# Gated values summed in place, output weights summed at their conversion, and the second FFN's operands loaded ahead of its first products

## The chip, the cores and the metric

The kernel runs on one core of a Trainium2 chip. A core has TensorE (PE, the matmuls), VectorE (DVE), ScalarE (ACT), GpSimd (POOL) and SyncE (SP, which here only issues DMAs), a scratch memory of 128 partitions (SBUF) and eight accumulation banks (PSUM). The metric is the device time of one execution in microseconds, as the median of some runs.

## The reference

The kernel computes three layers in a row, in float32:

```python
x = attention(q, k, v)              # 4 x 8 heads x 576 rows, window of 128, ALiBi bias -> x [2304, 512]
gate = 1 / (1 + exp(-(x @ w_gate))) # w_gate, w_val: [512, 1536]
val = x @ w_val
y = (gate * val) @ w_out            # w_out: [1536, 512]
# then a mixture of 8 experts, each token goes to the best one
out[mask] = gate_w[mask, None] * (relu(y[mask] @ w1[e]) @ w2[e])
```

w_gate, w_val and w_out arrive as 64-bit floats and are turned into 32-bit ones on the chip. Each float32 matmul operand is split into a high part and a low part (a rounding copy on ACT, a subtraction on DVE), and each product is three matmuls: high by high, high by low, low by high.

## The kernel before

The work comes in stages: attention; the first FFN matrices (gate and val) for a first pair of token chunks, interleaved with attention; the same for a second pair of chunks, called stage B here; the product with w_out; routing; the experts.

Stage B runs from about 290 to 440 us. It loops over 12 slices f of the 1536 hidden columns. For each f the 2 x 2 block product over the pair of chunks is done with seven products instead of eight (a Strassen form, lines 496 and on: m1 to m7), each of them six matmuls of 128 x 128 by 128 x 512. The seven products need sums of the token blocks (made once, held in 14 buffers) and, for each f, the weights W and sums of the weights T. Both come back from DRAM (`load_wt`, line 391), and are split by `split_w` (line 404): a cast to `wh` on ACT, then the subtraction on DVE, which writes the low part into the loaded buffer `wt`. In iteration f the weights of f + 1 are split and those of f + 2 are loaded. In the same iteration w_out's block f - 1 is converted (`split_wo`, line 740, by `split64`, line 136): an ACT multiplication, three integer operations on DVE, a store of the 32-bit block to DRAM (`wo_d`) by POOL's queue, and a split that stays in SBUF for the products to come.

The results of an iteration are gated in `keep_g` (line 441): `(tanh + 1) * val` on DVE, for two halves (chunks). For each pair of slices (f even, f odd; index kk) there are four blocks of gated values, A11 and A21 from the even f, A12 and A22 from the odd one. The product with w_out is again a seven-product form for these chunks, so POOL forms S1 = A21 + A22, S2 = S1 - A11, S3 = A21 - A11, S4 = A12 - S2, and seven blocks are stored to DRAM (`g7_d`) by POOL's queue. Before, the blocks and sums take four buffers for each kk: `gq` of the even f, `gq` of the odd f, and two of `sq`.

Buffers: nearly all of these operands are taken from one pool of 33 slots of 128 x 1024 floats (`NSLOT`, line 41, `slot(...)`), each given back when its last reader is done; a DMA or an engine that needs a slot waits for one. Smaller temporaries (`row(...)`) come from a pool of 10 rows of 128 x 528 floats (`NMID`, line 48). In stage B an iteration takes rows for c11, r1, c22 and c21 (the results of the products on their way to the gate) and one for w_out's block in conversion.

The order of the work: the program is written as Python loops, and a planner puts each engine's instructions in an order by their place in the program, their operands and free buffers, as it computes them ahead; every engine and queue then works strictly in that order. Where the code says `tc.manual_schedule(engines={...})`, the named engines keep the order of the program. Before, PE does so in the whole loop of stage B (line 805).

After stage B follows the product with w_out. The tokens of rows 4 and 3 (`ROWS = [4, 3, 2, 1, 0]`, 256 tokens each) go first, as plain products `mm2` with operands `gl`, `gh` (loaded from `gT_d`, split by `split_g`). Then `strassen` (line 1245) does the seven-product form for the second pair of chunks, in the order A11, S1, S2, S3, A22, S4, A12, with operands `ol`, `oh` (`load_op`, `split_op`) and the sums T of w_out (`tl`, `th`). Before, `prepare` (line 1282) brings these in: behind the products of row 4 it loads three of the six pairs of w_out blocks back from `wo_d`, sums them on POOL (four subtractions of 128 x 256 for each pair, line 1174), splits the sums, and loads the first operand; behind row 3 it does the other three pairs, then splits the first operand, loads the second and splits it.

A block of zeros (`zrow`, line 831) is stored to five places of the token table `x2_d` by POOL's queue at f = 3.

Of the kernel before, what the change touches and what calls it, by code (L numbers as in the profile page):

```python
# [9 lines left out]
F32 = mybir.dt.float32  # L10
F32R = mybir.dt.float32r
# [4 lines left out]
ALU = mybir.AluOpType  # L16
# [6 lines left out]
NT = B * S  # L23
DM = 512
FF = 1536
# [35 lines left out]
def attn_ffn_moe(ctx: ExitStack, tc: tile.TileContext, qkd, vd, wgv, w_out, emb, tau, w1, w2, cst, ids, out):  # L61
# [6 lines left out]
    wo_d = dram.tile([FF, DM], F32, tag="wo_d", name="wo_d")  # L68
# [49 lines left out]
    def lo_sub(eng, o, i, h):  # L118
        e = nc.vector if eng == "v" else nc.gpsimd
        e.tensor_tensor(out=o, in0=i, in1=h.bitcast(F32), op=ALU.subtract)  # L120
# [12 lines left out]
        nc.vector.scalar_tensor_tensor(out=yi, in0=hi, scalar=-2 ** 31, in1=yi, op0=ALU.bitwise_and,  # L133
                                       op1=ALU.bitwise_or)

    def split64(raw, wh, wl, nm, e2, keep):
        y = row(f"cv{nm}")[:, 0:512]
        conv64_a(raw, y)
        conv64_b(raw, y)
        nc.gpsimd.dma_start(keep, y)  # L140
        hi_copy("a", wh, y)
        lo_sub(e2, wl, y, wh)


    edge_pad = ctx.enter_context(tc.tile_pool(name="pad", bufs=1, side="right"))
# [245 lines left out]
    def load_wt(f):  # L391
        if f < KF:
            for z, (d, src) in list(enumerate(((wf, wf_d), (tf, tf_d))))[:1 if f < NC else 2]:
                t = slot([P, 2 * KD, P], F32R, f"wt{z}_{f}")
                d[f] = t.bitcast(F32)
                w_lo[f, z] = t
                nc.sync.dma_start(flat(d[f]), src[f * P:(f + 1) * P, :])
# [37 lines left out]
    gq, sq = {}, {}  # L435

    def g7_rows(name, kk, n=1):
        r = (NAMES.index(name) * KF // 2 + kk) * P
        return g7_d[r:r + n * P, :]

    def keep_g(f, half, gate, val):
        kk, odd = divmod(f, 2)
        if f not in gq:
            gq[f] = slot([P, 2, 512], F32, f"gq{f}")
        o = gq[f][:, half, :]
        nc.vector.scalar_tensor_tensor(out=o, in0=gate, scalar=1.0, in1=val, op0=ALU.add, op1=ALU.mult)  # L446
        if odd or not half:
            nc.gpsimd.dma_start(g7_rows(f"A{half + 1}{odd + 1}", kk), o)  # L448

        def put(name, t, x, y, op):  # L450
            nc.gpsimd.tensor_tensor(out=t, in0=x, in1=y, op=op)
            nc.gpsimd.dma_start(g7_rows(name, kk), t)

        a = gq[f - odd]
        if not odd and not half:
            sq[kk] = [slot([P, 2, 512], F32, f"sq{z}_{kk}") for z in range(1)]
            put("S3", sq[kk][0][:, 0, :], a[:, 1, :], a[:, 0, :], ALU.subtract)
        elif odd and half:
            sq[kk].append(slot([P, 2, 512], F32, f"sq1_{kk}"))
            put("S1", sq[kk][0][:, 1, :], a[:, 1, :], o, ALU.add)  # L460
            put("S2", sq[kk][1][:, 0, :], sq[kk][0][:, 1, :], a[:, 0, :], ALU.subtract)
        elif odd:
            put("S4", sq[kk][1][:, 1, :], o, sq[kk][1][:, 0, :], ALU.subtract)

    def piece(mm, ev):
        def both():
# [261 lines left out]

    op_ = ctx.enter_context(tc.tile_pool(name="op", bufs=8, side="right", reuse_waits="tile"))
    wo = []  # L730
    wo_raw = {}

    def load_wo(j):
        if j >= KF:
            return
        t = slot([P, 1024], I32, f"wor{j}")
        nc.sync.dma_start(t, w_out[j].bitcast(I32))
        wo_raw[j] = t

    def split_wo(j):  # L740
        if j % 3 == 0:
            wo.append(tuple(op_.tile([P, 3, DM], F32R, tag="c", name=f"wo{z}_{j}") for z in range(2)))
        h_, l_ = wo[-1]
        split64(wo_raw.pop(j), h_[:, j % 3, :], l_[:, j % 3, :], f"wo{j}", "v", wo_d[j * P:(j + 1) * P, :])

    def rnorm(ss, n, nm, w=P):
        s0 = sm.tile([P, n], F32, tag=f"sa{n}", name=f"sa_{nm}")[0:w, :]
# [54 lines left out]
    sv[0]["m2"]()  # L802
    bB["S3+"]()
    bB["S3"]()
    with tc.manual_schedule(engines={ENG.PE}):
        for f in range(KF):
            s, t = sv[f], sv[f + 1] if f + 1 < KF else None
            s["m5"]()
            if f == 0:
                bB["A22"]()  # L810
                bB["S4+"]()
            if f + 1 < NC:
                sum_w(f + 1, store=False)
            split_w(1, f + 1, 0)
            s["m6"]()
            if f == 0:
                bB["S4"]()
            if t:
                t["m1"]()
            s["m7"]()  # L820
            split_w(1, f + 1, 1)
            if t:
                t["m2"]()
            load_wt(f + 2)
            s["m4"]()
            if f:
                split_wo(f - 1)
            load_wo(f + 1)
            s["m3"]()
            if f == 3:  # L830
                zrow = row("zrow")
                nc.gpsimd.memset(zrow, 0.0)
                nc.gpsimd.dma_start(x2_d[NT:NT + 1, :], zrow[0:1, :])
                for b in LATE:
                    for u in range(2):
                        nc.gpsimd.dma_start(x2_d[(2 * b + u) * P:(2 * b + u + 1) * P, :], zrow)
            elif f == 7:
                load_emb()
            elif f == 9:
                norm_emb()  # L840
            elif f == 10:
                turn_emb()
    split_wo(KF - 1)


# [42 lines left out]
    idt = cp.tile([P, E * TCOL], I32, tag="idt", name="idt")  # L888
    nc.gpsimd.memset(idt, NT)
    nc.sync.dma_start(tab_d.rearrange("(p c) o -> p (c o)", p=P), idt)  # L890
    split_g(ROWS[0])
    tri = cp.tile([P, P], BF16, tag="tri", name="tri")
    nc.vector.tensor_copy(tri, tri_f)
# [268 lines left out]
    wt2 = {}  # L1162

    def load_w2(kk):
        t = slot([P, 2, DM], F32, f"wo32_{kk}")
        nc.sync.dma_start(t, wo_d[2 * kk * P:2 * (kk + 1) * P, :].rearrange("(z p) d -> p z d", p=P))
        wt2[kk] = t

    def sum_w2(kk):
        w = wt2.pop(kk)  # L1170
        b11, b12, b21, b22 = w[:, 0, 0:256], w[:, 0, 256:512], w[:, 1, 0:256], w[:, 1, 256:512]
        t = slot([P, 4, 256], F32, f"tq_{kk}")
        for z, (x, y) in enumerate(((b12, b11), (b22, t[:, 0, :]), (b12, b22), (b21, t[:, 1, :]))):
            nc.gpsimd.tensor_tensor(out=t[:, z, :], in0=x, in1=y, op=ALU.subtract)
        h_, l_ = (slot([P, 4, 256], F32R, f"t{z}_{kk}") for z in "hl")
        hi_copy("a", h_, t)
        lo_sub("v", l_, t, h_)
        wt2[kk, "T"] = h_, l_

    def w2_of(name, kk, z):  # L1180
        i = int(name[1:])
# [366 lines left out]
```

## Time and profile before

| | us |
|---|---|
| median of 3 runs | 894.05 |
| lowest, highest | 891.28, 894.74 |
| the profiled execution | 892.74 |
| its span (first to last instruction) | 890.8 |
| mean granted TensorE clock, share of full speed | 0.952 |

| engine | busy us | share of the span |
|---|---|---|
| PE | 816.2 | 92% |
| DVE | 595.3 | 67% |
| ACT | 459.3 | 52% |
| POOL | 264.2 | 30% |

A busy share is a mean over stages with different limits. Matmuls overlap, so a busy PE isn't PE at its peak. The granted clock is what TensorE ran at, as a share of its full 2.4 GHz. A wait is put down to the event that came last before the waiting instruction. In a row of the timeline "SPq" and "POOL ... DMA" are issues of DMAs; a DMA lands later.

### The profile page before, as it was taken

What the parts mean: (1) busy time and instruction counts of PE and PEld (TensorE: products, weight loads), DVE (VectorE), ACT (ScalarE), POOL (GpSimd) and SP (SyncE); (2) the same over time, 40 slices, a digit from 0 to 9 for tenths busy, and PEclk for the clock granted to TensorE, in tenths of its full rate; (3) what the DMA queues carried; (4) which work ended last, traced back from release to release, by engine and by line L of the source; (5) the groups of instructions that cost most, each with busy time, mean ns of one, the idle gap of its engine ahead of it and who ended that gap; (6) DMA issues with size and microseconds to landing.
All of it is one profiled execution on the core that took longest, in us unless ns stands there. A gap on an engine that the chain in (4) does not pass through costs nothing. (4 is left out here: it accounts for less than half of the span.)

```text
span 890.8 us, 15647 instructions
## 1 busy us (share of the span) xinstructions
PE 816.2 (92%) x5563; PEld 670.0 (75%) x5563; DVE 595.3 (67%) x1392; ACT 459.3 (52%) x956; POOL 264.2 (30%) x378
## 2 busy tenths in 40 slices
PE   9989999999999778786769699999899999999997
PEld 6768878888887556565557478777788999898796
DVE  7998787777997756676683566574574744645721
ACT  6897666665565323334343556873543543444410
POOL 6775322320001442334392210233122301210300
PEclk9999999999999878797879799999899999999999
DMA  8685656454535664563844358424348744544300
GB/s 272 188 280 190 231 192 207 154 184 171 210 120 215 209 214 138 192 208 123 294 165 137 113 177 278 170 73 157 93 130 272 274 166 145 188 171 137 132 22 17
DMA packets 68191, 156.13 MB, mean 175 GB/s; under 512 B 9191, under 2 KB 23271, under 8 KB 68112
## 3 DMA queue, kind: packets, MB, share of 16 engines
q1 hardware_dynamic: 58256, 125.59, 42.1%
q0 software_dynamic: 9856, 29.53, 9.2%
q8 instruction: 44, 0.72, 0.3%
q14 instruction: 35, 0.29, 0.1%
HBM read 110.96 MB, written 44.79 MB: 175 GB/s over the span
## 5 line engine op out<-in xcount | busy, mean ns | idle before, releaser
L1106 PE MATMUL h<-xe,weh 128*128 128x256 f32 (+4 forms) x512 | 107.7, 304 | 0.0
L116 POOL TENSOR_SCALAR p<-p,rs 128x192 f32<-128x192 f32 x140 | 76.3, 562 | 101.2 <-DVE rs L267 51.9
L1124 PE MATMUL z<-weh,h 128*128 128x512 f32 (+3 forms) x320 | 101.7, 397 | 0.9 <-DVE h L1109 0.6
L904 PE MATMUL y<-wo,gh 128*128 128x512 f32 x240 | 80.5, 407 | 11.1 <-ACT gh L104 11.1
L120 DVE TENSOR_TENSOR wel<-wer,weh 128x1024 fp32r<-128x1024 f32 x64 | 77.1, 1220 | 14.6 <-ACT weh L104 7.0
L1106 PEld LDWEIGHTS h<-xe,weh 128*128 128x128 f32 x512 | 85.8, 194 | 1.3 <-DVE h L1109 0.2
L1106 PE MATMUL h<-xe,wel 128*128 128x256 f32 (+4 forms) x256 | 77.7, 304 | 0.0
L251 ACT ACTIVATE p<-p,mx 128x192 f32<-128x192 f32 x144 | 64.0, 446 | 24.2 <-DVE mx L248 23.9
L104 ACT CAST weh<-wer 128x1024 fp32r<-128x1024 f32 x64 | 66.4, 1049 | 12.2 <-PE z L1124 9.7
L1129 POOL DMA_INDIRECT out<-y,cols x19 | 22.3, 1172 | 169.7 <-DVE y L1128 159.0
L1108 ACT ACTIVATE h<-h 128x256 fp32r<-128x256 f32 (+4 forms) x64 | 26.7, 417 | 81.3 <-PE h L1106 79.5
L1124 PEld LDWEIGHTS z<-weh,h 128*128 128x128 f32 (+3 forms) x320 | 56.6, 181 | 15.6 <-DVE h L1109 1.0
L448 POOL DMA_DIRECT2D g_d<-gq x18 | 10.3, 572 | 177.8 <-DVE gq L446 177.8
L1124 PE MATMUL z<-wel,h 128*128 128x512 f32 (+3 forms) x160 | 62.7, 392 | 0.0
L904 PEld LDWEIGHTS y<-wo,gh 128*128 128x128 f32 x240 | 45.7, 193 | 22.3 <-ACT gh L104 11.5
L1109 DVE SCALAR_TENSOR_TENSOR h<-h,h 128x256 fp32r<-128x256 f32 (+4 forms) x64 | 29.5, 463 | 47.0 <-ACT h L1108 46.8
L1106 PEld LDWEIGHTS h<-xe,wel 128*128 128x128 f32 x256 | 49.7, 194 | 0.0
L904 PE MATMUL y<-wo,gl 128*128 128x512 f32 x120 | 47.8, 399 | 1.8 <-DVE gl L120 1.8
L1128 DVE TENSOR_SCALAR y<-z,xg 128x512 f32<-128x512 f32 (+3 forms) x22 | 16.4, 747 | 49.2 <-PE z L1124 49.2
L1020 POOL DMA_INDIRECT tab_d<-ids_sb,ai x18 | 22.5, 1249 | 62.3 <-DVE xr L978 23.3
L527 DVE TENSOR_TENSOR c<-c,c 128x512 f32<-128x512 f32 x22 | 15.1, 686 | 33.7 <-ACT c L526 33.7
L248 DVE CUSTOM_DVE_ANT_0 p<-s,bias 128x192 f32<-128x192 f32 x96 | 30.6, 350 | 8.4 <-PE s L237 8.4
(450 smaller groups left out, 2264.5 us busy)
## 6 DMA issues: line engine op xcount, KB each, us to landing
wer<-in_w SPq DMA_DIRECT2D x64, 512.0 KB, 5.4
wr<-in_wgv SPq DMA_DIRECT2D x24, 512.0 KB, 5.3
qk<-in_qkd SPq DMA_DIRECT2D x36, 320.0 KB, 3.6
ol<-g_d SPq DMA_DIRECT2D x21, 512.0 KB, 4.0
gl<-gT_d SPq DMA_DIRECT2D x15, 512.0 KB, 8.6
v<-in_vd SPq DMA_DIRECT2D x36, 192.0 KB, 3.5
wf_d<-wf SPq DMA_DIRECT2D x12, 512.0 KB, 2.6
wt<-wf_d SPq DMA_DIRECT2D x12, 512.0 KB, 3.6
```

Source lines behind the costliest of these rows:

```text
L104: nc.scalar.copy(o, i)
L116: nc.gpsimd.tensor_scalar(out=t, in0=t, scalar1=r, scalar2=0.0, op0=ALU.mult, op1=ALU.add)
L120: e.tensor_tensor(out=o, in0=i, in1=h.bitcast(F32), op=ALU.subtract)
L248: nc.vector.tensor_tensor_reduce(out=o, in0=ss[u][:, j * WK:(j + 1) * WK], in1=bias, scale=-0.125, scalar=3.0e38, op0=ALU.add, op1=ALU.min ...
L251: nc.scalar.activation(out=o, in_=o, func=AF.Exp, scale=-1.0, bias=mx[:, z:z + 1], accum_out=su[:, z:z + 1])
L904: nc.tensor.matmul(m, g[:, k % 4, u * P:(u + 1) * P], w[:, k % 3, :], start=(k == 0 and z == 0), stop=(k == KF - 1 and z == 2))
L1020: nc.gpsimd.indirect_dma_start(out=tab_d, out_offset=IOA(ap=ai[:, u:u + 1], axis=0), in_=ids_sb[:, t:t + 1], in_offset=None)
L1106: nc.tensor.matmul(m[:, :n], w[:, fs], x[:, k, :], start=(cnt == 0), stop=(cnt == 3 * KD - 1))
L1108: nc.scalar.activation(out=hh, in_=m[:, :n], func=AF.Relu)
L1109: nc.vector.scalar_tensor_tensor(out=hl, in0=m[:, :n], scalar=0.0, in1=hh.bitcast(F32), op0=ALU.max, op1=ALU.subtract)
L1124: nc.tensor.matmul(m[0:w, :], h, ww[:, ds], start=(cnt == 0), stop=(cnt == 3 * KE - 1))
L1129: nc.gpsimd.indirect_dma_start(out=out, out_offset=IOA(ap=idx[0:w], axis=0), in_=y[0:w, :], in_offset=None, bounds_check=NT - 1, oob_is_er ...
```

## The change

`keep_g` takes one slot for each kk in place of four. Of the even f, A11 lies in its lower half (`low`), A21 in its upper half (`high`). Of the odd f, the gated values are written over the row that holds the tanh (`gate`), and stored from there. The sums are formed in place: S3 over A21, S2 as A22 plus S3, over S3, S1 as S2 plus A11, over A11, and S4 over A12 in its row.

`split64` no longer stores the 32-bit block of w_out; it hands its row back. At each odd block `split_wo` lets POOL form the four differences of the two rows in one slot and stores that slot to a new DRAM tensor `td_d`.

The loop of stage B is no longer under `manual_schedule`, so PE's order there is the planner's too; the statements in it are the same, but the zeros move behind the loop, behind the first loads of the product with w_out.

`load_op(0)` and the six loads of the sums stand ahead of the loop over rows. Behind row 4's products come the split of the first operand, the splits of the six sums (cast to a new slot, low part in place), and the load of the second operand; behind row 3's the split of the second operand.

```diff
-    def split64(raw, wh, wl, nm, e2, keep):
+    def split64(raw, wh, wl, nm, e2):
...
-        nc.gpsimd.dma_start(keep, y)
         hi_copy("a", wh, y)
         lo_sub(e2, wl, y, wh)
+        return y
...
     def keep_g(f, half, gate, val):
         kk, odd = divmod(f, 2)
-        if f not in gq:
-            gq[f] = slot([P, 2, 512], F32, f"gq{f}")
-        o = gq[f][:, half, :]
+        if not odd and kk not in gq:
+            gq[kk] = slot([P, 2, 512], F32, f"gq{kk}")
+        low, high = gq[kk][:, 0, :], gq[kk][:, 1, :]
+        o = gate if odd else (low, high)[half]
         nc.vector.scalar_tensor_tensor(out=o, in0=gate, scalar=1.0, in1=val, op0=ALU.add, op1=ALU.mult)
+
+        def put(name, t):
+            nc.gpsimd.dma_start(g7_rows(name, kk), t)
+
+        def sums(name, t, x, y, op):
+            nc.gpsimd.tensor_tensor(out=t, in0=x, in1=y, op=op)
+            put(name, t)
+
         if odd or not half:
-            nc.gpsimd.dma_start(g7_rows(f"A{half + 1}{odd + 1}", kk), o)
...
+            put(f"A{half + 1}{odd + 1}", o)
         if not odd and not half:
-            sq[kk] = [slot([P, 2, 512], F32, f"sq{z}_{kk}") for z in range(1)]
-            put("S3", sq[kk][0][:, 0, :], a[:, 1, :], a[:, 0, :], ALU.subtract)
+            sums("S3", high, high, low, ALU.subtract)
         elif odd and half:
-            sq[kk].append(slot([P, 2, 512], F32, f"sq1_{kk}"))
-            put("S1", sq[kk][0][:, 1, :], a[:, 1, :], o, ALU.add)
-            put("S2", sq[kk][1][:, 0, :], sq[kk][0][:, 1, :], a[:, 0, :], ALU.subtract)
+            sums("S2", high, o, high, ALU.add)
+            sums("S1", low, high, low, ALU.add)
         elif odd:
-            put("S4", sq[kk][1][:, 1, :], o, sq[kk][1][:, 0, :], ALU.subtract)
+            sums("S4", o, o, high, ALU.subtract)
...
-        split64(wo_raw.pop(j), h_[:, j % 3, :], l_[:, j % 3, :], f"wo{j}", "v", wo_d[j * P:(j + 1) * P, :])
+        wo_f[j] = split64(wo_raw.pop(j), h_[:, j % 3, :], l_[:, j % 3, :], f"wo{j}", "v")
+        if j % 2:
+            w = wo_f.pop(j - 1), wo_f.pop(j)
+            (b11, b12), (b21, b22) = ((y[:, 0:256], y[:, 256:512]) for y in w)
+            t = slot([P, 4, 256], F32, f"tq_{j}")
+            for z, (x, y) in enumerate(((b12, b11), (b22, t[:, 0, :]), (b12, b22), (b21, t[:, 1, :]))):
+                nc.gpsimd.tensor_tensor(out=t[:, z, :], in0=x, in1=y, op=ALU.subtract)
+            nc.gpsimd.dma_start(td_d[j // 2 * P:(j // 2 + 1) * P, :], t.rearrange("p z d -> p (z d)"))
...
-    with tc.manual_schedule(engines={ENG.PE}):
-        for f in range(KF):
+    for f in range(KF):
...
-            if f == 3:
-                zrow = row("zrow")
...
+    zrow = row("zrow")
+    nc.gpsimd.memset(zrow, 0.0)
...
     def load_w2(kk):
-        t = slot([P, 2, DM], F32, f"wo32_{kk}")
-        nc.sync.dma_start(t, wo_d[2 * kk * P:2 * (kk + 1) * P, :].rearrange("(z p) d -> p z d", p=P))
+        t = slot([P, 4, 256], F32R, f"tl_{kk}")
+        nc.sync.dma_start(t.bitcast(F32).rearrange("p z d -> p (z d)"), td_d[kk * P:(kk + 1) * P, :])
...
-    def sum_w2(kk):
...
+    def split_w2(kk):
+        t = wt2[kk]
+        h_ = slot([P, 4, 256], F32R, f"th_{kk}")
+        hi_copy("a", h_, t.bitcast(F32))
+        lo_sub("v", t, t.bitcast(F32), h_)
+        wt2[kk, "T"] = h_, t
...
-    def prepare(b):
-        if b == 0:
-            for kk in range(3):
-                load_w2(kk)
-                sum_w2(kk)
-            load_op(0)
-        elif b == 1:
-            for kk in range(3, 6):
-                load_w2(kk)
-                sum_w2(kk)
+    def prepare(i):
+        if i == 0:
             split_op(0)
+            for kk in range(6):
+                split_w2(kk)
             load_op(1)
+        elif i == 1:
             split_op(1)
 
+    load_op(0)
+    for kk in range(6):
+        load_w2(kk)
```

## Rows read from the trace of the kernel before

**Rows 1.** Windows: from:to, length, each engine's busy us, granted clock, DMA share, GB/s.
```profile
255.00:290.00 35.00, 34.30 (x163) 28.55 (x162) 28.68 (x38) 20.08 (x29) 4.51 (x5) 1.00 0.52 189
302.30:440.00 137.70, 106.94 (x372) 80.69 (x370) 90.86 (x106) 53.92 (x83) 46.64 (x62) 0.83 0.56 191
440.00:451.20 11.20, 0.13 (x1) 0.00 (x0) 10.23 (x12) 2.76 (x5) 8.07 (x11) 0.69 0.97 332
451.20:485.00 33.80, 31.99 (x140) 25.25 (x140) 19.91 (x32) 16.03 (x26) 19.80 (x18) 0.90 0.29 104
485.00:500.20 15.20, 7.07 (x39) 5.55 (x38) 6.82 (x20) 5.84 (x9) 8.11 (x10) 0.85 0.41 133
500.20:512.00 11.80, 11.80 (x40) 9.24 (x41) 8.21 (x9) 5.85 (x8) 0.00 (x0) 0.76 0.35 107
512.00:890.00 378.00, 369.56 (x2076) 313.59 (x2074) 209.91 (x533) 174.02 (x290) 77.91 (x77) 0.99 0.45 154
```

**Rows 2.** Timeline of PE: start, us, what; the product m5 opens an iteration.
```profile
302.30 0.39 PE L427 MATMUL c<-xh_(1, 'S1')_3829,wh 128*128 128x512 f32 x1
302.53 0.39 PE L427 MATMUL c<-xl_(1, 'S1')_3830,wh 128*128 128x512 f32 x1
...
431.03 0.50 PE L427 MATMUL c<-xh_(1, 'S1')_3829,wh 128*128 128x512 f32 x1
```

**Rows 3.** Waits of PE, 302.3 to 440 us: total us, times, longest.
```profile
PE a L427 <- DVE wt L120: 15.4, 8, 3.8
PE a L427 <- ACT wh L104: 14.1, 6, 5.1
```

**Rows 4.** Waits of the SP queue, same stretch.
```profile
SPq L397 <- PE a L427: 42.0, 3, 14.3
SPq L397 <- DMA g_d<-gq: 24.2, 3, 9.6
```

**Rows 5.** Timeline of DVE, 384 to 390 us.
```profile
384.41 1.86 DVE L131 SCALAR_TENSOR_TENSOR cvwo<-wor,cvwo 128x512 int32<-128x512 int32 x1
386.19 2.23 DVE L446 SCALAR_TENSOR_TENSOR gq<-c,r 128x512 f32<-128x512 f32 x1
388.34 0.68 DVE L133 SCALAR_TENSOR_TENSOR cvwo<-wor,cvwo 128x512 int32<-128x512 int32 x1
388.95 1.21 DVE L120 TENSOR_TENSOR wt<-wt,wh 128x1024 fp32r<-128x1024 f32 x1
```

**Rows 6.** Timeline of POOL beside it.
```profile
384.41 1.29 POOL L451 TENSOR_TENSOR sq<-gq,gq 128x512 f32<-128x512 f32 x1
...
386.58 1.27 POOL L451 TENSOR_TENSOR sq<-sq,gq 128x512 f32<-128x512 f32 x1
```

**Rows 7.** Timeline of ACT, 440 to 500 us; in brackets what it waited for.
```profile
450.12 5.77 ACT L104 CAST gh<-gl 128x1024 fp32r<-128x1024 f32 x6
...
491.96 1.04 ACT L104 CAST th<-tq 128x1024 fp32r<-128x1024 f32 x1 [7.16 <-POOL tq L1174]
```

**Rows 8.** Waits of PE, 440 to 502 us.
```profile
PE y L904 <- ACT gh L104: 11.1, 1, 11.1
PE a L1218 <- ACT oh L104: 5.9, 1, 5.9
```

**Rows 9.** DMA issues, 302.3 to 440 us: KB each, median us to landing.
```profile
g_d<-gq POOLq DMA_DIRECT2D x13, 256.0 KB, 2.7
```

**Rows 10.** POOL's sums by line: ns least/median/most, first and last start.
```profile
L451 POOL TENSOR_TENSOR sq<-gq,gq x6: 1273/1294/1300, 288.5 to 441.0; 128x512 f32<-128x512 f32 x6
...
L1174 POOL TENSOR_TENSOR tq<-wo x12: 728/742/1719, 451.0 to 495.9; 128x256 f32<-128x256 f32 x12
```

**Rows 11.** DVE's operations by line, 300 to 452 us.
```profile
L537 DVE TENSOR_TENSOR r<-r,c x10: 677/680/689, 302.7 to 440.4; 128x512 f32<-128x512 f32 x10
...
L446 DVE SCALAR_TENSOR_TENSOR gq<-c,r x10: 681/1452/2394, 303.9 to 442.8; 128x512 f32<-128x512 f32 x10
...
L130 DVE TENSOR_SCALAR cvwo<-cvwo x11: 412/419/422, 302.4 to 445.5; 128x512 int32<-128x512 int32 x11
```

More of the change, by code (lines that the diff above doesn't have):

```diff
@@ L67, in attn_ffn_moe @@
     g7_d = dram.tile([7 * FF // 2, 512], F32, tag="g7_d", name="g7_d")
-    wo_d = dram.tile([FF, DM], F32, tag="wo_d", name="wo_d")
+    td_d = dram.tile([FF // 2, 1024], F32, tag="td_d", name="td_d")
     x2_d = dram.tile([NT + 1, DM + 1], F32, tag="x2_d", name="x2_d")
@@ L434, in attn_ffn_moe @@
     NAMES = ["A11", "A12", "A22", "S1", "S2", "S3", "S4"]
-    gq, sq = {}, {}
+    gq = {}
     def g7_rows(name, kk, n=1):
@@ L442, in keep_g @@
         kk, odd = divmod(f, 2)
-        if f not in gq:
-            gq[f] = slot([P, 2, 512], F32, f"gq{f}")
-        o = gq[f][:, half, :]
+        if not odd and kk not in gq:
+            gq[kk] = slot([P, 2, 512], F32, f"gq{kk}")
+        low, high = gq[kk][:, 0, :], gq[kk][:, 1, :]
+        o = gate if odd else (low, high)[half]
         nc.vector.scalar_tensor_tensor(out=o, in0=gate, scalar=1.0, in1=val, op0=ALU.add, op1=ALU.mult)
-        if odd or not half:
-            nc.gpsimd.dma_start(g7_rows(f"A{half + 1}{odd + 1}", kk), o)
[L450 to L454, printed above, removed]
+        def put(name, t):
[3 more added lines that the diff above has]
+            put(name, t)
+        if odd or not half:
+            put(f"A{half + 1}{odd + 1}", o)
         if not odd and not half:
-            sq[kk] = [slot([P, 2, 512], F32, f"sq{z}_{kk}") for z in range(1)]
-            put("S3", sq[kk][0][:, 0, :], a[:, 1, :], a[:, 0, :], ALU.subtract)
+            sums("S3", high, high, low, ALU.subtract)
         elif odd and half:
-            sq[kk].append(slot([P, 2, 512], F32, f"sq1_{kk}"))
-            put("S1", sq[kk][0][:, 1, :], a[:, 1, :], o, ALU.add)
-            put("S2", sq[kk][1][:, 0, :], sq[kk][0][:, 1, :], a[:, 0, :], ALU.subtract)
+            sums("S2", high, o, high, ALU.add)
+            sums("S1", low, high, low, ALU.add)
         elif odd:
-            put("S4", sq[kk][1][:, 1, :], o, sq[kk][1][:, 0, :], ALU.subtract)
+            sums("S4", o, o, high, ALU.subtract)
     def piece(mm, ev):
@@ L730, in attn_ffn_moe @@
     wo = []
-    wo_raw = {}
+    wo_raw, wo_f = {}, {}
     def load_wo(j):
@@ L804, in attn_ffn_moe @@
     bB["S3"]()
-    with tc.manual_schedule(engines={ENG.PE}):
-        for f in range(KF):
[L807 to L829, printed above, removed]
-            if f == 3:
-                zrow = row("zrow")
[L832 to L842, printed above, removed]
+    for f in range(KF):
+        s, t = sv[f], sv[f + 1] if f + 1 < KF else None
+        s["m5"]()
+        if f == 0:
+            bB["A22"]()
+            bB["S4+"]()
+        if f + 1 < NC:
+            sum_w(f + 1, store=False)
+        split_w(1, f + 1, 0)
+        s["m6"]()
+        if f == 0:
+            bB["S4"]()
+        if t:
+            t["m1"]()
+        s["m7"]()
+        split_w(1, f + 1, 1)
+        if t:
+            t["m2"]()
+        load_wt(f + 2)
+        s["m4"]()
+        if f:
+            split_wo(f - 1)
+        load_wo(f + 1)
+        s["m3"]()
+        if f == 7:
+            load_emb()
+        elif f == 9:
+            norm_emb()
+        elif f == 10:
+            turn_emb()
     split_wo(KF - 1)
@@ L890, in attn_ffn_moe @@
     nc.sync.dma_start(tab_d.rearrange("(p c) o -> p (c o)", p=P), idt)
+    zrow = row("zrow")
+    nc.gpsimd.memset(zrow, 0.0)
+    nc.gpsimd.dma_start(x2_d[NT:NT + 1, :], zrow[0:1, :])
+    for b in LATE:
+        for u in range(2):
+            nc.gpsimd.dma_start(x2_d[(2 * b + u) * P:(2 * b + u + 1) * P, :], zrow)
     split_g(ROWS[0])
@@ L1164, in load_w2 @@
     def load_w2(kk):
-        t = slot([P, 2, DM], F32, f"wo32_{kk}")
-        nc.sync.dma_start(t, wo_d[2 * kk * P:2 * (kk + 1) * P, :].rearrange("(z p) d -> p z d", p=P))
+        t = slot([P, 4, 256], F32R, f"tl_{kk}")
+        nc.sync.dma_start(t.bitcast(F32).rearrange("p z d -> p (z d)"), td_d[kk * P:(kk + 1) * P, :])
         wt2[kk] = t
-    def sum_w2(kk):
[L1170 to L1178, printed above, removed]
+    def split_w2(kk):
[4 more added lines that the diff above has]
+        wt2[kk, "T"] = h_, t
     def w2_of(name, kk, z):
```

## The prediction

> **What bounds the kernel now.** I read the page's 40 slices first. PE is at 9 tenths or more nearly everywhere but in the middle, from slice 13 to slice 23, and the changed code lies there. Windows cut at the seams of the stages put sizes to it [rows 1]. From 512 us on PE is busy 369.6 of 378.0 us at clock 0.99: nothing is to be won there, and what the middle gains or loses goes into the total unshortened. The opening of stage B is full too (34.3 of 35.0 us, clock 1.00). Then come 137.7 us with PE busy 106.9 and clock 0.83, 11.2 us with PE at rest, 33.8 us at clock 0.90, 15.2 us with PE busy 7.1, and 11.8 us at clock 0.76. All the time in question is there.
>
> An iteration of stage B should take PE 42 matmuls at 0.23 us, 9.6 us. Eight iterations lie between the m5 at 302.30 and the one at 431.03, so each takes 16.1 us [rows 2]. Of the 6.5 us too many, waiting is 29.5 us over the stretch, some 3.4 an iteration: PE stands at m1 of the next slice, whose weights wait for the DVE subtraction or the ACT cast [rows 3]. The other 3.1 are the clock, which falls between its levels of 2.4 and 1.2 GHz when PE has stood.
>
> Why are the weights late? Two causes show. The first is slots: SP's reloads of the weights wait until PE gives slots back (42.0 us), or until a store out of gq has read its slot (24.2 us) [rows 4]. Count them: 14 for the token blocks, 4 for the slice in use, 4 for the next, 2 loaded ahead, 2 or 3 raw w_out blocks, and up to 4 of gq and sq: 30 or 31 of 33, before a slot that only waits for its store to land. The second is DVE's queue. In an odd iteration two DVE operations of 0.68 us take 1.86 and 2.23, and the subtraction of the next weights stands behind them [rows 5]; POOL sums of 1.29 and 1.27 us run at those very times [rows 6]. The two exclude each other: 1.86 less 0.68 is nearly one POOL sum.
>
> Behind stage B, PE waits 11.1 us for the first cast of gh, and later 5.9 us for oh [rows 8]. Six gh casts start at 450.12, behind w_out's last two blocks; the casts of th wait up to 7.16 us for POOL's sums of w_out, and oh stands behind them [rows 7].
>
> **The change, part by part.**
>
> *Gated values in place.* Per pair of slices POOL still makes four sums (1.29 us each, 5.2 us) and seven stores; work is neither added nor removed. Four slots become one, freeing two to three of 33 at the fullest time. One wait is added: S4 overwrites the row from which A12 was just given to a store, so POOL must wait for it, median 2.7 us [rows 9]. Behind it on POOL's queue stand S4's own store and w_out's sums; nobody on PE's path reads them in stage B, so I cost it at nothing. Its cover is the row pool: the rows of c21 and c11 of an odd slice are held longer, by sums and stores.
>
> *Sums of w_out at conversion.* Twelve stores of 256 KB become six of 512 KB; 24 sums of 128 x 256 move from 451 to 498 us into stage B, at 0.73 us alone and 1.72 beside a busy DVE [rows 10]. That is four per pair, 2.9 to 6.9 us of POOL, right after the DVE operation that completes the odd block, thus just where the next weights' subtraction stands in line. A row of the even block is held an iteration longer.
>
> What floor does this set? DVE's work in a pair of slices, at its least durations: eight gate and integer operations and two w_out subtractions of 0.69, six additions out of PSUM of 0.69, two integer ones of 0.42 and four weight subtractions of 1.21: 16.7 us [rows 5, 11]. POOL's sums: 5.2 + 2.9 = 8.1. If every sum stops DVE for its length, a pair takes 24.8 us, 12.4 an iteration (before: 10.9). But one row speaks for less: the addition that reads PSUM never took over 0.689 us in ten, while the gate that reads two SBUF tiles took 0.68 to 2.39 [rows 11]. Counting only operations of the second sort (ten of 0.69 and four of 1.21, 11.7 us), the floor is 9.9, close to PE's 9.6.
>
> [...]
>
> *PE's order by the planner.* No instruction is added. Where the planner sees m1 late it can put m7, m2, m4 or m3 ahead, or products of row 4, whose operands don't depend on stage B. No row prices this. From below it can win all 3.4 us of waiting and the 3.1 of clock per iteration; from above it can lose, since an order made for undisturbed operations meets disturbed ones.
>
> *Sum for stage B.* The pace lies between 9.9 and, were every moved sum added to the path, 16.1 + 2.9/2 = 17.6 us. I take 14.2, the middle between the row of now (16.1) and the plain floor (12.4): slots are freed, but DVE's queue is longer. Eight iterations by 1.9 give -15.
>
> *The end of stage B.* 11.2 us of rest and 33.8 x 0.10 = 3.4 us of low clock, 14.6 in all [rows 1]. With loads of gl nearer and PE's order free, row 4's products can fill the rest; against it, the last two blocks of w_out still come on ACT ahead of gh, and the moved zeros (four stores of 256 KB) and more loads meet a DMA share of 0.97. Bounds 0 and -14.6; I take half, -7.
>
> *The start of the seven-product form.* The first operand's loads are issued ahead of row 4's products and its split no longer stands behind sums, so oh can be there before row 3's last product. ACT has 15 casts to do by then (six gh, six th, three oh, 15.6 us at 1.04) and DVE 15 subtractions (18.2 at 1.21), in the 34 us of rows 4 and 3, in which ACT is busy 16.0 us and DVE 19.9 now, much of it these very splits, and without POOL's sums beside them. Slots: 12 for rows 4 and 3, 12 for the sums, 6 for the first operand, 30 of 33, and six come back after row 4. Gone are the rest from 485.0 to 500.2 (15.2 - 7.1 = 8.1) and the low clock after it (11.8 x 0.24 = 2.8): -11. Bounds 0 (loads are late all the same) and -11. Next late would be the second operand, whose loads come behind the first's splits.
>
> *Total.* The profiled execution took 892.7 us, 1.9 of them outside its span. 892.7 - 15 - 7 - 11 = 859.7; it lies 1.3 under the median of the runs, so the forecast is 861.
>
> **The rivals.**
>
> *Slower: the moved sums land on DVE's path.* Each of the 24 stands between the completed block and the next weights' subtraction. At 0.73 us all on the path they cost 17.5; if the freed slots and PE's order bring nothing and the end of stage B stays, only the 11 at the start of the form is gained: 892.7 + 17.5 - 11 + 1.3 = 901. At 1.72 each it would be 924. It decides from a pace of 17.5 us on, where stage B costs the 11 that the form gains. For it: rows 5 and 6 show just this happening with the sums there are. Against: 14.1 of the 29.5 us are waits for the ACT cast, which POOL can't lock out [rows 3], so the lockout isn't the only cause. Chance 0.16.
>
> *Both causes go: a pace of 9.9 to 12.4.* Stage B then gains 30 to 50, the end 14.6, the form 11: 818 to 838, the latter by the plain floor. For it: the opening of stage B ran at 34.3 of 35.0 with slots to spare. Against: POOL was busy only 4.5 us in it. Chance 0.21. [...]
>
> *Only the start of the form gains.* Slots that fall free are taken at once by loads from further ahead (gl, the sums, the first operand), which hold them to the end, and the weights are as late as before: 892.7 - 11 + 1.3 = 883. Chance 0.17.
>
> *The rows run short.* Ten rows must now hold two blocks of w_out, two odd gates and the five rows in motion. If the copy of the next c11 waits 2.7 us in each of six pairs, and as much again is lost to the clock (3.1 beside 3.4 now), 32 us go: 861 + 32 = 893, no change. Chance 0.08.
>
> **How the numbers follow.** Forecast, 848 to 876: 0.38. Under 848: 0.21. 876 to 889.6: 0.17. Within 0.5% of 894.05, about what a measurement can tell from no change (889.6 to 898.5): 0.08. Above: 0.16. Faster is 0.76. The range 830 to 899 leaves out the lower end of the second rival (0.04) and the slower one (0.16).
>
> **What would show it.** In the trace after, m5 starts should lie some 14 us apart; PE's waits for wt and wh in stage B should fall below 20 us; the gap before the first gh cast should halve; the first matmul of the form should follow row 3's last one without rest, and no th cast should wait for POOL. DVE operations with two SBUF inputs should show more stretched ones, with w_out's 24 sums beside them. It is wrong if the pace is over 16 or under 12, if SP's waits for slots stay as they are, or if PE gets a new wait for a row (c11 or r1 behind a store).

## The result and the profile after

The changed kernel takes 846.48 us in the median of three runs (845.42 to 847.95), the kernel before 894.05 us: a ratio of 0.948, 95% interval 0.944 to 0.952. It is faster by 47.6 us; the forecast was 33 (861 us), the range 830 to 899. The time lies just under the 848 to 876 us of the likeliest case, in the band below 848 us that the prediction gave to "both causes go" (chance 0.21). The profiled span fell from 890.8 to 846.1 us, the mean granted clock rose from 0.952 to 0.981.

Windows of the trace after, cut at its own seams, in the columns of [rows 1]; the seam that was at 451.20 us is now at 420.50, the form that began at 500.20 begins at 458:

```profile
298.53:410.60 112.07, 92.85 (x372) 71.78 (x370) 92.02 (x107) 53.85 (x84) 70.40 (x75) 0.94 0.69 240
410.60:420.50 9.90, 0.45 (x3) 0.01 (x1) 8.45 (x10) 2.25 (x4) 7.76 (x10) 0.67 0.90 345
...
470.00:845.00 375.00, 366.96 (x2057) 311.61 (x2056) 204.75 (x506) 169.47 (x282) 77.53 (x75) 0.99 0.45 153
```

The timeline of PE after, the products that open iterations 3 and 11 (m5), as in [rows 2], and the first matmul of the seven-product form:

```profile
298.53 0.39 PE L427 MATMUL c<-xh_(1, 'S1')_3829,wh 128*128 128x512 f32 x1
...
396.26 0.50 PE L427 MATMUL c<-xh_(1, 'S1')_3829,wh 128*128 128x512 f32 x1
...
457.90 0.40 PE L910 MATMUL y<-wo,gh 128*128 128x512 f32 x1
458.14 0.62 PE L1220 MATMUL a<-oh,wo 128*128 128x512 f32 x2
```

Eight iterations take 97.73 us, 12.2 each (before 16.1), and the form follows row 3 without rest. With these seams the 44.7 us come apart (starts of the first product of row 4: 451.22 and 420.49 us; of the form: 500.15 and 458.14):

| stretch | before | after | difference | forecast |
|---|---|---|---|---|
| up to the m5 of iteration 3 | 302.3 | 298.5 | -3.8 | 0 |
| eight iterations | 128.7 | 97.7 | -31.0 | -15 |
| from there to row 4's first product | 20.2 | 24.2 | +4.0 | -5.6 |
| rows 4 and 3, up to the form | 48.9 | 37.7 | -11.3 | -9.8 |
| from the form's start to the end | 390.7 | 388.0 | -2.7 | -2.8 |

The forecast's terms are laid on these seams by their own rows: half of the 11.2 us of rest in the third stretch, half of the 3.4 us of low clock and the 8.1 us of rest in the fourth, the 2.8 us of low clock behind the form's start in the last.

The eight iterations alone, before and then after, one window of each (columns of [rows 1]):

```profile
302.30:431.03 128.73, 99.30 (x342) 75.19 (x340) 84.28 (x97) 50.97 (x77) 43.72 (x58) 0.81 0.55 186
```

```profile
298.53:396.26 97.73, 83.14 (x342) 64.61 (x340) 84.32 (x97) 50.31 (x78) 61.53 (x63) 0.97 0.65 227
```

The same 342 matmuls took PE 99.30 us and then 83.14: 16.2 us of the gain lie in the matmuls themselves, with the granted clock at 0.97 in place of 0.81 of full speed. The time in which PE did nothing fell from 29.4 to 14.6 us, another 14.8. DVE's busy time didn't change (84.28, 84.32), though POOL's rose by 17.8 us beside it.

PE's waits after, 298 to 411 us (first three rows, for [rows 3]) and 410 to 502 us (the last, for [rows 8]):

```profile
PE c L427 <- DVE c L528: 8.7, 4, 2.2
PE a L427 <- DVE wt L120: 4.9, 4, 1.7
PE a L427 <- ACT c L527: 4.8, 3, 3.8
...
PE y L910 <- ACT gh L104: 9.5, 1, 9.5
```

The wait for the weights' cast is gone (14.1 before), that for their subtraction is 4.9 (15.4). The largest is new: 8.7 us for a sum behind the products, before a later one may overwrite its bank. The wait for gh is nearly as long as it was (11.1); that for oh (5.9) is gone.

SP's waits in the eight iterations after, for [rows 4]:

```profile
SPq L397 <- DVE cvwo L133: 28.4, 6, 9.9
SPq L397 <- DMA g_d<-gq: 22.1, 4, 7.2
```

The reloads of the weights (line 397) still wait for slots, 52.6 us in all against 79.8, and for a store of gated values as long as before (22.1 against 24.2 us), though PE hardly waits for weights any more. A sum of waits on a queue that runs ahead says little.

ACT after stage B, for [rows 7]: the casts of w_out's last two blocks wait for DVE, and the gh casts stand behind them, as before.

```profile
415.57 0.62 ACT L104 CAST wo<-cvwo 128x512 fp32r<-128x512 f32 x1 [5.31 <-DVE cvwo L133]
418.87 0.62 ACT L104 CAST wo<-cvwo 128x512 fp32r<-128x512 f32 x1 [2.69 <-DVE cvwo L133]
419.40 2.94 ACT L104 CAST gh<-gl 128x1024 fp32r<-128x1024 f32 x3
```

### The profile page after: what moved, and what is told of

Same layout as the page of the kernel before. It is cut to its first block, busy times and chain, and to the rows that moved or that the text cites. A ratio compares the mean times of both kernels' runs of the same rounds, so it can differ in the third digit from the quotient of the medians.

```text
span 846.1 us, 15609 instructions
## 1 busy us (share of the span) xinstructions
PE 797.2 (94%) x5563; PEld 657.3 (78%) x5563; DVE 586.9 (69%) x1392; ACT 458.2 (54%) x956; POOL 269.1 (32%) x372
## 5 line engine op out<-in xcount | busy, mean ns | idle before, releaser
L251 ACT ACTIVATE p<-p,mx 128x192 f32<-128x192 f32 x144 | 64.0, 446 | 24.2 <-DVE mx L248 24.0
L910 PEld LDWEIGHTS y<-wo,gh 128*128 128x128 f32 x240 | 45.4, 192 | 20.8 <-ACT gh L104 10.2
L1115 DVE SCALAR_TENSOR_TENSOR h<-h,h 128x256 fp32r<-128x256 f32 (+4 forms) x64 | 29.5, 464 | 46.0 <-ACT h L1114 45.9
L1134 DVE TENSOR_SCALAR y<-z,xg 128x512 f32<-128x512 f32 (+3 forms) x22 | 16.4, 747 | 49.2 <-PE z L1130 45.5
L450 POOL DMA_DIRECT2D g_d<-gq x24 | 13.6, 568 | 90.1 <-PE a L427 79.7
L120 DVE TENSOR_TENSOR wt<-wt,wh 128x1024 fp32r<-128x1024 f32 x22 | 34.8, 1611 | 2.1 <-ACT wh L104 2.0
```

The source lines that it names most:

```text
L251: nc.scalar.activation(out=o, in_=o, func=AF.Exp, scale=-1.0, bias=mx[:, z:z + 1], accum_out=su[:, z:z + 1])
L910: nc.tensor.matmul(m, g[:, k % 4, u * P:(u + 1) * P], w[:, k % 3, :], start=(k == 0 and z == 0), stop=(k == KF - 1 and z == 2))
L1115: nc.vector.scalar_tensor_tensor(out=hl, in0=m[:, :n], scalar=0.0, in1=hh.bitcast(F32), op0=ALU.max, op1=ALU.subtract)
```

## The experiments

All ratios are to the kernel before, with 95% intervals. "Pace" is the time of one iteration, from the m5 of iteration 3 to that of iteration 11, divided by eight.

**One part at a time.** The change has three separable parts: the sums in place, PE's order left to the planner, and the w_out part (sums at the conversion, sooner loads, later zeros). Each was put into the kernel before by itself, and the first two together.

In place alone (`keep_g` of the changed kernel, the rest as before):

```diff
-        if f not in gq:
-            gq[f] = slot([P, 2, 512], F32, f"gq{f}")
-        o = gq[f][:, half, :]
+        if not odd and kk not in gq:
+            gq[kk] = slot([P, 2, 512], F32, f"gq{kk}")
+        low, high = gq[kk][:, 0, :], gq[kk][:, 1, :]
+        o = gate if odd else (low, high)[half]
```

> The kernel before with the gated values summed in place alone (one slot in place of four for each pair of slices); PE's order by hand, w_out's sums and the loads as before. Slots theory: the weights' casts come sooner, the pace of an iteration of stage B falls from 16.1 to about 14 us, total about 877 us. Order theory (PE's order alone brings the gain in stage B): pace stays at 16, total 890 to 896.

846.11 us, 0.947 [0.944, 0.949]: the whole gain of the change, by this part alone, 31 us under the lower of the two expectations.

PE's order by the planner, alone (`with tc.manual_schedule(engines={ENG.PE}):` taken off the loop):

> The kernel before with PE's order in stage B left to the planner, nothing else changed. Slots theory: the weights are as late as before, PE can fill a part of the waits; pace 14.5 to 16, total 880 to 893. Order theory: pace about 12.2 as in the changed kernel, total about 863.

872.07 us, 0.977 [0.973, 0.980], pace 13.2: between the two theories, borne out by neither.

Both:

> The kernel before with both, sums in place and PE's order by the planner; w_out's sums, zeros and loads as before. Slots theory: pace 12 or less, since POOL's 24 sums aren't in stage B; the form's start stays late; total about 858 to 863. Theory that the moved sums cost nothing: pace 12.2, total about 862.

844.65 us, 0.945 [0.942, 0.947], 13 us under what was expected: with the sums in place the order adds nothing that can be told.

The w_out part alone, with four slots for a pair and PE by hand:

> The kernel before with the rest of the change alone: w_out's sums on POOL at the conversion, loads and splits of the seven-product form's operands sooner, zeros later; gated values in four slots, PE's order by hand. The form's start gains 11 us; the 24 sums lengthen stage B by 0 (cost nothing) to 17 us (all on DVE's path): total 883 to 900; I expect 890.

885.27 us, 0.991 [0.988, 0.994], within the range. The eight iterations in these four kernels, in this order:

```profile
300.90:388.44 87.54, 80.01 (x342) 62.29 (x340) 73.65 (x97) 50.08 (x78) 46.62 (x58) 1.00 0.83 277
```

```profile
304.40:410.26 105.86, 86.89 (x343) 62.88 (x341) 84.00 (x97) 50.56 (x78) 43.62 (x58) 0.97 0.66 224
```

```profile
299.11:386.70 87.59, 81.29 (x342) 63.55 (x340) 77.45 (x97) 50.01 (x78) 45.93 (x58) 0.98 0.82 273
```

```profile
303.76:434.98 131.22, 97.00 (x341) 74.02 (x339) 92.31 (x97) 50.94 (x77) 51.09 (x64) 0.82 0.48 170
```

In place alone has the pace at 10.9 us, the clock at full speed and DVE 10.6 us less busy than before. The w_out part alone leaves the pace at 16.4 and makes DVE 8.0 us busier; its gain is at the start of the form (from the m5 of iteration 11 to the form 58.9 us, before 69.1). The parts don't add up: 47 + 21 + 8 us alone, 48 together.

In place alone and the whole change take the same time, but not in the same places. Cut at the seams of the table above, in place alone takes 300.9, 87.5, 10.6, 55.8 and 389.4 us. It is 10.2 us faster than the whole change in the eight iterations and 13.7 us at the end of stage B, and 18.2 us slower in rows 4 and 3, where the form waits 11.5 us for oh.

**Whether it is free slots.** The in-place kernel with three slots fewer (`NSLOT = 30`):

> The kernel before with the sums in place alone (it took 846), and with 30 slots in place of 33. The 33 slots of the kernel before held six slots of gated values for two pairs; in place they hold two and so three or four more are free at any time. If stage B gains because of these free slots, taking three of them away brings the waits for them back: the iterations go from 10.9 us to 14 or more, SP's wait for the store of gated sums is back, and the time is over 870 us. If the gain came from the shorter chain of sums (fewer slots asked for, at a time that no longer depends on POOL), three slots less cost little: 846 to 852 us, iterations of 11 to 11.5 us. If it is free slots over a threshold, between the two.

862.65 us, 0.967 [0.965, 0.969]: between the two by its time, but not by its place. The pace is 11.0, as with 33 slots; of the 15.8 us of span 4.5 were lost up to the start of the form, where PE waits 13.5 us for oh (11.5 with 33), and 11.3 behind it. SP's and PE's waits in its eight iterations:

```profile
SPq L397 <- PE a L427: 52.6, 6, 10.0
```

```profile
PE a L427 <- DVE wt L120: 4.6, 4, 2.0
```

With three slots fewer the reloads of the weights wait 54.4 us for slots in all, with 33 slots 18.9, and the pace is the same; PE hardly waits for weights in either. By my own count of the slots, this kernel has about as few to spare as the kernel before. So the number of free slots, which the prediction named first, isn't what set the pace.

The trace of the kernel before says so too. SP issues a reload, and ACT casts these weights together with those loaded just ahead of them (loads and casts paired in their order):

```profile
351.33 0.38 SPq L397 DMA_DIRECT2D wt<-tf_d  x1
```

```profile
370.14 0.62 ACT L104 CAST wo<-cvwo 128x512 fp32r<-128x512 f32 x1 [2.93 <-DVE cvwo L133]
...
371.14 1.99 ACT L104 CAST wh<-wt 128x1024 fp32r<-128x1024 f32 x2
```

All 14 casts from 325 us on start at least 20.2 us behind the issue of their reload, which lands 3.3 to 4.8 us after its issue. The reloads had landed long before; no wait for a slot made these casts late.

What made them late is their place in ACT's queue. In these rows the casts stand behind the cast of a w_out block, which waits for DVE to finish converting that block. The in-place kernel:

```profile
366.81 1.99 ACT L104 CAST wh<-wt 128x1024 fp32r<-128x1024 f32 x2
369.85 0.62 ACT L104 CAST wo<-cvwo 128x512 fp32r<-128x512 f32 x1 [1.05 <-DVE cvwo L133]
...
370.85 1.05 ACT L104 CAST wh<-wt 128x1024 fp32r<-128x1024 f32 x1
```

Before, 13 of the 16 weight casts of eight iterations stand behind the cast of a w_out block. In five iterations both casts do, and PE waits 13.9 us for the casts and 4.4 us for the subtractions behind them. In the other three the first cast comes in time, but its subtraction stands on DVE behind the same conversion, beside POOL's sums as in [rows 5, 6], and PE waits 10.9 us for it. One wait of PE of each kind:

```profile
372.25 0.50 PE L427 MATMUL a<-xh_(1, 'A11')_3795,wh 128*128 128x512 f32 x1 [2.20 <-ACT wh L104]
```

```profile
359.13 0.79 PE L427 MATMUL a<-xh_(1, 'A11')_3795,wt 128*128 128x512 f32 x1 [3.48 <-DVE wt L120]
```

So 18.3 of the 29.5 us stand on ACT's order and 10.9 on DVE's, and both go back to the conversion of w_out. In the in-place kernel the four casts of a pair lie in one iteration, two ahead of the w_out cast and two behind it, and the other iteration has none: half of the weights are ready an iteration sooner. The kernel with 30 slots has the very same sequence. The wait itself, by ACT's groups of lines in eight iterations (busy us, mean ns, then the idle time ahead), before and in place:

```profile
L104 ACT CAST wo<-cvwo 128x512 fp32r<-128x512 f32 x8 | 4.9, 618 | 29.7 <-DVE cvwo L133 29.7
```

```profile
L104 ACT CAST wo<-cvwo 128x512 fp32r<-128x512 f32 x8 | 5.0, 621 | 10.9 <-DVE cvwo L133 9.1 <-DVE sa_e L750 1.8
```

Every kernel here with the sums in place and a pace under 12.3 us has its casts two ahead and two behind; the three with four slots for a pair don't. Where PE's order is by hand, the order of the casts and the pace go together. But order alone has 13 of 16 casts behind w_out's as before, with the wait ahead of these at 10.5 us, and a pace of 13.2. An order of ACT written out by hand over the four slots wasn't tried, so that this order by itself sets the pace is argued and not shown; why the planner orders the casts otherwise when the sums are in place stays open. A rival, that DVE has less to do (10.6 us in place alone), can't explain the first step, since the whole change has DVE as busy as before at a pace of 12.2. For the second it stands untested: the kernels with the sums in place run at 11.0 us or less where DVE is busy for under 78 us in the eight iterations, and at 11.8 or more where it is over 82.

**What the w_out part costs in stage B.** In place alone runs at 10.9 us, the whole change at 12.2. First, the 24 subtractions became memsets of the same tiles (the sums T are left out of the result):

```diff
-                nc.gpsimd.tensor_tensor(out=t[:, z, :], in0=x, in1=y, op=ALU.subtract)
+                nc.gpsimd.memset(t[:, z, :], 0.0)
```

> The changed kernel with each of w_out's 24 subtractions on POOL in place of a memset of the same size, which reads nothing (the sums T of w_out are left out). Port theory (POOL's sums that read SBUF stop DVE in stage B): the pace falls from 12.2 to about the 10.9 that the kernel with sums in place alone shows, total 834 to 840. Rows and slots theory (the longer-held rows and slots cost it): pace and total as in the changed kernel, 844 to 848.

842.32 us, 0.942 [0.939, 0.944], and the pace stays at 12.2: not confirmed for the eight iterations. The 4 us come behind them: row 4 starts 12.2 us after the m5 of iteration 11, with the sums 24.2. In its eight iterations DVE is as busy as with the sums, and POOL has 20 us less:

```profile
298.74:396.51 97.77, 82.28 (x341) 64.77 (x340) 84.26 (x97) 49.54 (x78) 41.77 (x64) 0.97 0.68 232
```

Now POOL's gated sums meet other instructions, as this subtraction of weights on DVE, alone 1.21 us, and the sum on POOL beside it:

```profile
352.99 2.71 DVE L120 TENSOR_TENSOR wt<-wt,wh 128x1024 fp32r<-128x1024 f32 x1
```

```profile
353.34 1.28 POOL L453 TENSOR_TENSOR gq<-gq 128x512 f32<-128x512 f32 x1
```

Two more rows of temporaries (`NMID = 12`, and 32 slots to make room):

> The changed kernel with 12 rows and 32 slots in place of 10 and 33. Rows theory: the copies that wait for a store out of a row go (3 to 4 us in the last iteration, some in the ones before): total 838 to 843. Port theory: 845 to 848, or a little more for the slot that is gone.

843.42 us, 0.943 [0.941, 0.945], pace 12.0, the new wait for the sum behind the products unchanged (9.1 us). So rows don't set the pace. But in the last iteration ACT no longer waits for a store out of a row, and from its m5 to row 4's first product it takes 21.4 us in place of 24.2. That is about the 3 us by which the time is lower, though the two intervals still touch.

The last two of this kind start from the fastest kernel, told below (836.4 us, pace 10.9, w_out's sums in the form), and add one half of the w_out part each. Rows held until the odd block has come:

```diff
-        nc.gpsimd.dma_start(keep, y)
+        if j % 2:
+            for i in (j - 1, j):
+                nc.gpsimd.dma_start(wo_d[i * P:(i + 1) * P, :], wo_f.pop(i))
```

> The in-place sums with PE's order by the planner and the first operand of the second FFN loaded ahead (836 us), and one thing of the w_out part added: the converted row of an even block of w_out is held until the odd block has come, and both are stored then. No further sums. If it is the held rows that lengthen the iterations of the changed kernel from 10.9 to 12.2 us, they lengthen them here: 12 us or more, 845 us or more. If it is the 24 sums of POOL and their slot, the iterations stay at 10.9 us and the time at 835 to 838 us.

834.16 us, 0.935 [0.933, 0.938], pace 10.7: held rows cost nothing that can be told. And four extra differences of each odd row, with their slot and store:

> The same 836 us kernel with the other half of the w_out part added: at each odd block of w_out POOL forms four differences of 128x256 into a slot, from halves of the odd row alone, and stores them to DRAM, where nothing reads them; no row is held longer than these take, and the sums in the seven-product form stay. If POOL's sums and their slot lengthen the iterations (to 12 us), the time is 845 us or more; if the held rows do, it stays at 836 to 839 us. If neither does alone, it is both together.

849.61 us, 0.951 [0.948, 0.954], pace 13.0. The eight iterations of the kernel that both start from, then with rows held, then with sums added:

```profile
299.85:386.82 86.97, 80.26 (x341) 62.27 (x340) 77.92 (x97) 49.79 (x78) 43.20 (x58) 1.00 0.82 275
```

```profile
297.98:383.42 85.44, 80.34 (x342) 62.28 (x340) 76.42 (x97) 49.82 (x78) 43.08 (x58) 1.00 0.83 281
```

```profile
297.63:401.55 103.92, 86.02 (x341) 65.84 (x339) 86.91 (x97) 48.99 (x77) 58.02 (x78) 0.93 0.71 247
```

The job on POOL is the cost: 13 us of time, and 17 in the eight iterations (103.92 against 86.97); that is more than the 10.2 us of the whole change, where the stores of w_out's blocks are gone. It makes DVE 9.0 us busier (77.92 to 86.91); in the whole change against in place alone it is 10.7. Since memsets in the sums' place left the pace at 12.2, their reading of SBUF alone isn't it; how much is their slot and store, which reorder the rest, stays open.

**The end of stage B.** In place alone starts row 4 10.6 us after the m5 of iteration 11 (before 20.2, the whole change 24.2). There the planner put the first cast of gh ahead of w_out's last two blocks on ACT, and PE waits little for it:

```profile
PE y L905 <- DVE gl L120: 4.9, 1, 4.9
...
PE y L905 <- ACT gh L104: 1.4, 1, 1.4
```

With the four differences added at each odd block (849.61 us) the wait for gh is back at 8.4 us. So the sums of the w_out part take back at this seam what the sums in place had won. An order by hand was tried on the changed kernel, the conversions of w_out's blocks 10 and 11 traced behind the split of gh:

```diff
-    split_wo(KF - 1)
...
     split_g(ROWS[0])
+    split_wo(KF - 2)
+    split_wo(KF - 1)
```

> The changed kernel with the conversion of w_out's last two blocks written behind the split of row 4's first operands. If ACT's order alone holds the gh casts back at the end of stage B, the wait of 9.5 us there goes: total about 838. If the casts have no slot before, or row 4's products wait for the late blocks, 844 to 848.

846.06 us, 0.946 [0.944, 0.949]: no gain. PE's waits around the seam (in brackets what it waited for):

```profile
409.12 0.74 PE L911 MATMUL y<-wo,gh 128*128 128x512 f32 x2 [0.20 <-ACT gh L104]
414.90 0.80 PE L911 MATMUL y<-wo,gl 128*128 128x512 f32 x1 [5.04 <-DVE gl L120]
```

Row 4 starts 11.4 us sooner, but then waits 5.0 us for the subtraction of gl, and rows 4 and 3 take 45.0 us in place of 37.7: the form starts 4.0 us sooner, and the time doesn't show it. The wait went on in part to DVE's queue, which was busy for 8.45 of the 9.90 us at this seam in the changed kernel.

**The start of the form.** The sums in place, PE's order by the planner, w_out's sums in the form as before, and only the first operand moved:

```diff
+    load_op(0)
     def prepare(b):
         if b == 0:
+            split_op(0)
             for kk in range(3):
                 load_w2(kk)
                 sum_w2(kk)
-            load_op(0)
```

(and the split taken out of the later branch)

> Sums in place and PE's order by the planner (844.65 us), and of the rest only the load of the form's first operand ahead of the rows and its split behind row 4; w_out's sums stay where they were before. The wait of 11.8 us for oh goes, stage B keeps its pace of 10.9: total about 834. If the sums T are then late for the second product: 838 to 843.

836.44 us, 0.936 [0.934, 0.937], between the two outcomes: 10 us under the changed kernel. With its two relatives of 834.2 and 836.2 us, whose intervals overlap its own, it is the fastest found. The form starts at 439.83 us without rest; with in place and order alone PE waited 11.8 us there for oh. PE next waits for the second operand:

```profile
452.85 0.79 PE L1218 MATMUL c<-oh,th 128*128 128x512 f32 x1 [3.65 <-ACT oh L104]
```

That one moved ahead of the last three sums too:

> The 836 us kernel with the second operand of the second FFN loaded behind the first three sums of w_out and split ahead of the last three, in place of behind all six. In the 836 us kernel PE waits 3.6 us for its casts, which stand behind those of th, which wait for POOL's sums. If this wait is all that the order costs, it goes: 831 to 833 us. If the casts of th for the last three blocks become late in its place, or the operands' other casts (ol), the time is 835 to 838 us.

836.21 us, 0.937 [0.935, 0.939]: no gain, the second of the two outcomes. Its wait is gone, and th is late in its place, whose casts wait for POOL's sums either way:

```profile
453.96 0.79 PE L1218 MATMUL c<-oh,th 128*128 128x512 f32 x1 [1.73 <-ACT th L104]
```

## Why the prediction was right, and where its terms failed

The time moved the way that was forecast and lies in the range, but the terms missed in opposite directions: stage B won 16 us more than forecast, its end lost 10 us against the forecast, and 3.8 us came ahead of iteration 3, where nothing was forecast. That the total is off by 14.5 us and not by more is luck.

*Stage B, -15 forecast, -31 measured.* The direction and the place were right, and the waits for the weights fell from 29.5 us to 4.9, under the 20 that the prediction set as its sign. The term that failed is the pace, "the middle between the row of now (16.1) and the plain floor (12.4): slots are freed, but DVE's queue is longer". DVE's time didn't become longer: 84.28 and 84.32 us in eight iterations. In place alone takes 10.6 us off DVE, the w_out part gives 10.7 back. And the lost clock goes with the waiting: 14.8 us of PE's idle time and 16.2 us of clock went together. A middle between bounds treated as a mixture what was one coupled loss. That the pace came out near the plain floor (12.2 against 12.4) doesn't bear that floor out: with memsets, which read nothing, in place of w_out's sums it is 12.2 as well, and other kernels here run under the plain floor of 10.9 for the work before. This is the rival "both causes go" in its pace, but not in its total, since the end of stage B didn't follow.

*The cause.* "The first is slots" isn't borne out: with 30 slots the pace holds, and before, the reloads had landed long ahead of their casts. The second cause, DVE's queue ahead of the next weights, was real (10.9 of the 29.5 us), but seen on DVE alone; the larger part (18.3) was ACT's queue, where the casts stood behind one that waits for DVE. The prediction read that PE waited for an ACT cast [rows 3], took this for a sign that DVE wasn't the only cause, and didn't ask what that cast stood behind. So the gain came by another way than the one that was priced first.

*The end of stage B, -5.6 of the -7 forecast, +4.0 measured.* From the m5 of iteration 11 to row 4's first product the bound of 0 was passed, before and then after:

```profile
431.03:451.22 20.19, 7.78 (x34) 5.50 (x32) 16.83 (x21) 5.73 (x10) 11.01 (x15) 0.83 0.88 302
```

```profile
396.26:420.49 24.23, 10.15 (x33) 7.17 (x32) 16.14 (x21) 5.77 (x10) 16.62 (x21) 0.74 0.91 334
```

PE's idle time grew by 1.7 us, and its busy time by 2.4 us at a lower granted clock. The wait for gh went only from 11.1 to 9.5 us, for the reason that was written against the gain (w_out's last blocks ahead of gh on ACT). Without the w_out part these blocks weren't ahead of it, and the term came out: -9.6 in place alone. New is the wait for a row that was named as a sign of failure. It shows once, in the last iteration:

```profile
404.91 0.58 ACT L527 COPY c<-a 128x512 f32<-128x512 f32 x1 [3.17 <-DMA g_d<-c]
```

ACT's copy waits for a store out of a row, and PE stands 3.8 us. "The rows run short" priced this six times; it happened once. The other sign, SP's waits for slots, fell by a third (79.8 to 52.6 us), but the run with 30 slots shows that they tell nothing of the pace.

*The start of the form, -11 forecast.* The form follows row 3 without rest, no cast of th waits for POOL. By the seams of the table -9.8 and then -2.8 were forecast, -11.3 and -2.7 measured: this term was right in size and in its mechanism. Rows 4 and 3, before and then after:

```profile
451.22:500.15 48.93, 39.00 (x178) 30.74 (x178) 26.66 (x52) 21.80 (x35) 27.89 (x28) 0.88 0.33 113
```

```profile
420.49:458.14 37.65, 37.43 (x169) 29.70 (x170) 26.67 (x47) 23.66 (x34) 6.85 (x9) 0.94 0.49 147
```

*The moved sums.* The slower rival was right that they cost time in stage B, and wrong in their weight. Against in place alone the w_out part costs 1.3 us an iteration and 13.7 at the end of stage B, and brings 18.2 in rows 4 and 3. That it is by lockouts, as the rival has it, the memsets don't bear out for the iterations. Of the change's three parts one gives it all, and the w_out part pays in stage B for what it wins behind it. The prediction never priced the three apart.

*Lockouts.* DVE operations with two SBUF inputs are stretched beside w_out's sums as forecast; but so is one with a single SBUF input, which the floor of 9.9 left out. DVE in the trace after, first its integer operation on w_out, then three weight subtractions of 1.21 us each:

```profile
323.10 1.53 DVE L130 TENSOR_SCALAR cvwo<-cvwo 128x512 int32<-128x512 int32 x1
...
354.70 5.66 DVE L120 TENSOR_TENSOR wt<-wt,wh 128x1024 fp32r<-128x1024 f32 x3
```

and POOL beside them:

```profile
322.61 1.72 POOL L453 TENSOR_TENSOR c<-c,gq 128x512 f32<-128x512 f32 x1 [3.10 <-ACT c L531]
...
355.34 1.71 POOL L751 TENSOR_TENSOR tq<-cvwo,tq 128x256 f32<-128x256 f32 x1
357.02 2.26 POOL L453 TENSOR_TENSOR gq<-gq 128x512 f32<-128x512 f32 x1
```

The integer operation took 0.42 us at all times before [rows 11]; here it ends 0.3 us after the sum. The Trainium skill ("SBUF — State Buffer", section "Who interferes with whom") lists this sort too: a tensor_scalar in a mode that uses both port pairs takes the shared one. The row agrees, and 0.42 us against 0.68 for the two-input operations of its size fits such a mode. Two more operations of 0.42 us in a pair put the floor at 10.3 us in place of 9.9; the changed kernel ran at 12.2.

## What to carry to other kernels

When PE waits for a cast or a copy, look at what stands ahead of it on that engine: in a queue that works strictly in order, a piece of side work that waits for another engine holds up everything behind it. Where waiting drags the clock down, price the two together, since they go together. And try each part of a change alone: here one of three held the whole gain, and the version that leaves w_out's sums where they were and loads the first operand sooner is 10 us faster than all three.

## What the runs showed of the hardware that was not expected

- One SBUF input doesn't free a DVE operation from POOL: 0.42 us alone, 1.53 beside a POOL sum.
- POOL pays as well: a gated sum of 1.29 us took 4.08 in the in-place kernel, beside one subtraction of w_out (0.68) and two of weights (2.35 for two), all at their full speed:

```profile
326.44 4.08 POOL L453 TENSOR_TENSOR c<-c,gq 128x512 f32<-128x512 f32 x1 [5.12 <-ACT wo L104]
```

- Which of the two loses isn't fixed. In eight iterations of in place alone POOL's 16 gated sums take 24.6 us (20.6 at 1.29 each) and DVE is busy for 73.7; with memsets among them the sums take 20.7 us and DVE 84.3, though all 16 memsets take only 4.4.
